# Windowed attention and a GELU network in one kernel: the division of the exponentials on GpSimd in all batches, their halves by one instruction over a range

## The chip, the core and the metric

The kernel runs on one core of a Trainium2 chip. The metric is the device time of one execution in microseconds. The kernel before was timed in three runs: 938.73, 940.12 and 943.64 us, median 940.12. One more execution was recorded by the hardware profiler.

## The reference, cut to what matters

Eight batches of eight heads attend over 576 tokens, each token to itself and the 127 before it, with a linear bias per head. The result goes through a network of two matrix products with a GELU between them.

```python
scores = scale * q @ k.T                         # B=8, H=8, S=576, D=64
scores = where((rel >= 0) & (rel < 128), scores - slope[h] * |rel|, -1e9)
attn = exp(scores - max(scores)); attn = attn / (sum(attn) + 1e-9)
x = (attn @ v).reshape(B * S, 512)
h = x @ w_in                                     # 512 x 2048
out = (0.5 * h * (1 + erf(h / sqrt(2)))) @ w_out # 2048 x 512
```

All of it is in float32. The kernel keeps that precision on 16-bit products: a number is split into a high half (its float16) and a low half (what is left, again float16), and a product takes three matrix products, high by high, high by low and low by high.

## The kernel before, in words

A batch has four units, one for each pair of heads. A unit's scores are nine groups of 128 rows by 192 keys, written s (two buffers). They fall into two ranges, EVEN with five groups and ODD with four; a range is the grain of the softmax.

**The softmax of batch 0** (`softmax_first`, L460 to L481). TensorE makes the scores in float32; VectorE takes the maxima (L469); ScalarE takes the exponentials with their sums z (L475); VectorE adds 1e-9 and inverts z (L478, L479) and multiplies each group by its 1/z (L481), into `e_main` for units 0 and 2 and into the space of `vbuf` for units 1 and 3. `turn` then transposes a unit's nine groups on TensorE (L496, with filler products of L490 ahead) and ScalarE evicts them to `et` (L498). `weigh` multiplies by v (`av`, L559), ScalarE writes the high half of `x` (L572) and VectorE the low half (`low_part`, recorded as L149).

**The softmax of the other batches** (`softmax`, L500 to L524). The exponentials go back into s in place (L510). In batches 1 and 2 ScalarE writes the high halves, one group at a time (L517); from batch 3 on GpSimd does (L519). VectorE computes the low halves, one group at a time, s * (1/z) - high (L149). Both halves go to `e_main`, of which there is one, and a DMA transposes each range to `et` (L522).

**Weights.** While batch 0's attention runs, the eight pieces of w_in come by DMA as 64-bit words. ScalarE and VectorE turn them into float32 (`zi`; ScalarE L190 and L192, VectorE L195, L196, L199) and split them into halves `wi` (ScalarE L207, VectorE L149). For the scale of two pieces their largest magnitudes are reduced over the partitions by GpSimd (`partition_all_reduce`, L114, in four steps called stw, one for each two pieces; in the listings they are stw_659, stw_686, stw_715 and stw_744). The same reduction serves v of batch 0 (stv) ahead of them, and q, k, v of batch 1 and w_out (stq, stv, stwo) after them. VectorE takes each result up in L115.

**The network.** Tile t is 512 tokens. `mlp_in` (L600) makes 16 blocks h of features from x; ScalarE applies GELU (L626 from tile 1 on), GpSimd and VectorE make the halves (L627, L149); `mlp_out` (L661) makes the output. In tile 0 the halves are made without GpSimd. The attention of batch b is laid between the steps of tile b - 1. The last two tiles use a form with seven products in place of eight.

**What sets the order.** The program is written in the order of the source with priorities, and a scheduler lays out each engine's queue before the run. Each engine then works through its queue strictly in that order. GpSimd has its routines in two libraries: `partition_all_reduce` is in library 1, `tensor_scalar` in library 0, and memset needs neither. Where the queue goes from a routine of one library to one of the other, the builder puts in an instruction that exchanges the library. In the listings it is a row `ISA` without a tile; the profile has it as MODIFY_POOL_CONFIG, in two parts. Before, the queue exchanges twice: to library 1 ahead of stv, and back to library 0 ahead of the first L627 in tile 1.

Of the kernel before, what the change touches and what calls it, by code (L numbers as in the profile page):

```python
# [14 lines left out]
AF = mybir.ActivationFunctionType  # L15
ALU = mybir.AluOpType
# [42 lines left out]
def attention_gelu_mlp(  # L59
# [10 lines left out]
    nc = tc.nc  # L70
# [389 lines left out]
    def softmax_first(st):  # L460

        u, s = st.u, st.s
        st.nmax = nmax = small([P, NG], f"nmax{u}", 2, tag="nmax")
        st.z = z = small([P, NG], f"z{u}", 2, tag="z")
        e = e_first[st.hp % 2]
        st.et = et = pool.tile([P, NG * 2, P], F32, tag=f"et{st.hp % 2}", name=f"et{u}", bufs=1)
        for r, c, banks in ((EVEN, slice(0, W), BANKS[0:3]), (ODD, slice(QB, 256), BANKS[3:5])):
            for bank in banks:
                nc.vector.tensor_reduce(  # L469
                    out=nmax[:, bank[0] : bank[-1] + 1], in_=st.ps[bank][:, 0 : len(bank), 0:W], axis=AX.X,  # L470
                    op=ALU.max, negate=True,
                )
            for bank in banks:
                for n, i in enumerate(bank):
                    nc.scalar.activation(  # L475
                        s[:, i, :], st.ps[bank][:, n, 0:W], AF.Exp, bias=nmax[:, i : i + 1], accum_out=z[:, i : i + 1]
                    )
            nc.vector.tensor_scalar_add(z[:, r], z[:, r], 1e-9)  # L478
            nc.vector.reciprocal(z[:, r], z[:, r])  # L479
            for i in range(r.start, r.stop):  # L480
                nc.vector.tensor_scalar_mul(e[:, i, c], s[:, i], z[:, i : i + 1])  # L481

    def turn(st):

# [15 lines left out]
    def softmax(st):  # L500
        u, s = st.u, st.s
        st.nmax = nmax = small([P, NG], f"nmax{u}", 2, tag="nmax")
        st.z = z = small([P, NG], f"z{u}", 2, tag="z")
        e = e_main
        st.et = et = pool.tile([P, NG * 4, P], F16, tag=f"et{st.hp % 2}", name=f"et{u}", bufs=1)
        for r, c, banks in ((EVEN, slice(0, W), BANKS[0:3]), (ODD, slice(QB, 256), BANKS[3:5])):
            nc.vector.tensor_reduce(out=nmax[:, r], in_=s[:, r], axis=AX.X, op=ALU.max, negate=True)  # L507
            with tc.high_priority(EXP_AHEAD):
                for i in range(r.start, r.stop):
                    nc.scalar.activation(  # L510
                        s[:, i, :], s[:, i, :], AF.Exp, bias=nmax[:, i : i + 1], accum_out=z[:, i : i + 1]
                    )
            nc.vector.tensor_scalar(z[:, r], z[:, r], 1e-9, 2.0 ** -E_SHIFT, op0=ALU.add, op1=ALU.mult)
            nc.vector.reciprocal(z[:, r], z[:, r])
            for i in range(r.start, r.stop):
                if st.b < 3:
                    nc.scalar.activation(e[:, i, 0, c], s[:, i], AF.Copy, scale=z[:, i : i + 1])  # L517
                    continue
                nc.gpsimd.tensor_scalar(e[:, i, 0, c], s[:, i], z[:, i : i + 1], 1.0, op0=ALU.mult, op1=ALU.mult)  # L519
            for i in range(r.start, r.stop):  # L520
                low_part(e[:, i, 1, c], s[:, i], z[:, i : i + 1], e[:, i, 0, c])
            nc.sync.dma_start_transpose(  # L522
                et[:, r.start * 4 : r.stop * 4, :], e[:, r].rearrange("p g h k -> p (g h k)")
            )  # L524
# [601 lines left out]
    for t in range(1, NTILE):  # L1126
# [26 lines left out]
        for step in range(2 * NFC):  # L1153
# [8 lines left out]
            if step in at:  # L1162
                hp, i = at[step]
# [63 lines left out]
```

## Time and profile before

| | us |
|---|---|
| median of three runs | 940.12 |
| lowest and highest run | 938.73, 943.64 |
| span of the profiled execution, first to last instruction | 936.4 |
| TensorE busy in it | 900.2 |
| VectorE busy | 737.2 |
| ScalarE busy | 555.9 |
| GpSimd busy | 199.0 |

The runs' times are whole executions, while the span goes from the first instruction to the last; the profiled execution's own whole time isn't listed apart. The median lies 3.7 us above the span, and that is taken as what lies around it. In rows of the profile, PE is TensorE, PEld its loading of weights, DVE VectorE, ACT ScalarE, POOL GpSimd and SP the engine that issues the DMAs; a q behind a name is the engine's queue. A row of the timeline has its start, its duration, engine, line, operation, written tile and read tiles, shapes and count, and in brackets the idle time before it with what ended it. A row of groups has count, busy time and the mean duration of one in ns. A row of windows has the stretch and its length, then the busy time of each engine with its instructions.

### The profile page before, as it was taken

What the parts mean: (1) busy time and instruction counts of PE and PEld (TensorE: products, weight loads), DVE (VectorE), ACT (ScalarE), POOL (GpSimd) and SP (SyncE); (2) the same over time, 40 slices, a digit from 0 to 9 for tenths busy, and PEclk for the clock granted to TensorE, in tenths of its full rate; (3) what the DMA queues carried; (4) which work ended last, traced back from release to release, by engine and by line L of the source; (5) the groups of instructions that cost most, each with busy time, mean ns of one, the idle gap of its engine ahead of it and who ended that gap; (6) DMA issues with size and microseconds to landing.
All of it is one profiled execution on the core that took longest, in us unless ns stands there. A gap on an engine that the chain in (4) does not pass through costs nothing.

```text
span 936.4 us, 18792 instructions
## 1 busy us (share of the span) xinstructions
PE 900.2 (96%) x7500; PEld 487.0 (52%) x7500; DVE 737.2 (79%) x1445; ACT 555.9 (59%) x1175; POOL 199.0 (21%) x412
## 2 busy tenths in 40 slices
PE   7969999779999899999999999999999999999998
PEld 3544444434454445444454445444444444488887
DVE  6898989779876877678767877687646898999771
ACT  5977958777673566256435643575465545744760
POOL 1010000013201443135303531164114540000000
PEclk9989999999999999999999999999999999999999
DMA  9518433872456133614562446224402351001001
GB/s 319 215 46 298 173 107 74 199 203 57 86 137 157 36 66 78 197 36 76 97 164 69 62 102 176 69 51 83 104 13 51 71 84 46 1 12 35 1 1 46
DMA packets 173512, 91.26 MB, mean 97 GB/s; under 512 B 132592, under 2 KB 155248, under 8 KB 173296
## 3 DMA queue, kind: packets, MB, share of 16 engines
q1 hardware_dynamic: 173424, 90.06, 38.6%
q8 instruction: 59, 0.97, 0.4%
q14 instruction: 29, 0.24, 0.1%
HBM read 46.53 MB, written 9.44 MB: 60 GB/s over the span
## 4 chain that ended last, share of the span: by engine, by line
PE 53%; DVE 19%; ACT 8%; DMA 4%; issue 3%; SPq 1%; POOL 0%; POOLq 0%; DVEq 0%; ACTq 0%
PE o L661 22%; PE h L600 17%; PE av L559 3%; PE sc L415 3%; DMA v<-vp 2%; ACT s L510 2%; PE u L860 2%; PE u_out L947 2%; DVE g L149 2%; DVE e_main L149 2%; DVE nmax L507 1%; PE v L860 1%; DMA et<-e_main 1%; DVE stv L217 1%; DVE s L437 1%
## 5 line engine op out<-in xcount | busy, mean ns | idle before, releaser
L600 PE MATMUL h<-x,wi 128*128 128x512 f16 x1536 | 341.1, 380 | 6.1 <-ACT g L626 3.1
L600 PEld LDWEIGHTS <-wi 128*128 128x128 f16 x1536 | 147.5, 98 | 184.7 <-issue 9.0
L661 PE MATMUL o<-wo,g 128*128 128x512 f16 x936 | 213.0, 380 | 1.1 <-DVE wo L149 1.1
L661 PEld LDWEIGHTS <-g 128*128 128x128 f16 x1248 | 117.2, 98 | 141.5 <-issue 2.3
L510 ACT ACTIVATE s<-s,nmax 128x192 f32<-128x192 f32 x252 | 111.2, 442 | 96.9 <-DVE nmax L507 93.3
L627 POOL TENSOR_SCALAR g<-g,sg 128x512 f16<-128x512 f32 x96 | 77.9, 817 | 192.0 <-ACT g L626 189.8
L149 DVE SCALAR_TENSOR_TENSOR e_main<-s,z,e_main 128x192 f16<-128x192 f32 x252 | 107.0, 468 | 13.1 <-POOL e_main L519 8.9
L519 POOL TENSOR_SCALAR e_main<-s,z 128x192 f16<-128x192 f32 x180 | 93.0, 534 | 86.9 <-issue 31.3
L626 ACT ACTIVATE g<-h,gs 128x512 f32<-128x512 f32 x96 | 63.9, 687 | 74.5 <-PE h L600 51.8
L149 DVE SCALAR_TENSOR_TENSOR g<-g,sg,g 128x512 f16<-128x512 f32 (+1 forms) x112 | 90.3, 824 | 21.0 <-POOL g L627 19.4
L415 PE MATMUL sc<-kbuf,qbuf 64*64 64x192 f16 (+1 forms) x1656 | 74.8, 263 | 9.2 <-DMA kbuf<-kp 4.5
L437 DVE SCALAR_TENSOR_TENSOR s<-sc,cs,bias_h 128x384 f32<-128x384 f32 x112 | 63.8, 608 | 12.2 <-PE sc L415 12.0
L661 PE MATMUL o<-wo_first,g 128*128 128x512 f16 x312 | 71.8, 379 | 0.1
L507 DVE TENSOR_REDUCE nmax<-s 128x5 f32<-128x960 f32 (+1 forms) x56 | 58.6, 1046 | 2.2 <-POOL s L442 0.2
L442 POOL MEMSET s<- 64x128 f32 (+1 forms) x112 | 19.1, 171 | 186.7 <-DVE s L437 186.1
L572 ACT ACTIVATE x<-av,cx 128x448 f16<-128x448 f32 (+6 forms) x52 | 23.5, 474 | 58.0 <-PE av L559 57.9
L415 PEld LDWEIGHTS <-qbuf 64*64 64x64 f16 x1512 | 36.0, 106 | 38.4 <-issue 36.9
L559 PE MATMUL av<-et,vbuf 128*64 128x128 f16 (+1 forms) x1680 | 44.1, 211 | 6.4 <-DMA et<-e_main 6.3
L559 PEld LDWEIGHTS <-vbuf 128*64 128x64 f16 x1680 | 41.0, 111 | 16.6 <-issue 11.3
L510 ACT ACTIVATION_READ_ACCUMULATOR s<-s,nmax 128x1 f32 x252 | 47.1, 187 | 0.0
L510 ACT ACT_TABLE_LOAD x29 | 37.2, 1283 | 7.9 <-DVE square L120 7.4
L947 PEld LDWEIGHTS <-g 128*128 128x128 f16 x384 | 37.6, 98 | 4.6
(268 smaller groups left out, 1159.7 us busy)
## 6 DMA issues: line engine op xcount, KB each, us to landing
v<-vp SPq DMA_DIRECT2D x32, 320.0 KB, 5.5
out<-ob SPq DMA_DIRECT2D x34, 256.0 KB, 2.3
raw<-w_in SPq DMA_DIRECT2D x8, 1024.0 KB, 13.7
raw<-w_out SPq DMA_DIRECT2D x8, 1024.0 KB, 5.1
q<-qp SPq DMA_DIRECT2D x7, 1152.0 KB, 6.2
k<-kp SPq DMA_DIRECT2D x7, 1152.0 KB, 6.3
qbuf<-qp SPq DMA_DIRECT2D x4, 288.0 KB, 4.9
kbuf<-kp SPq DMA_DIRECT2D x4, 288.0 KB, 5.2
```

Of the source, the lines that this page charges most:

```text
L149: nc.vector.scalar_tensor_tensor(out=dst, in0=src, scalar=scale, in1=high, op0=ALU.mult, op1=ALU.subtract)
L415: nc.tensor.matmul(ps[bank][o, n, 0:W], a, m, start=(i == 0), stop=(i == len(terms) - 1 and b > 0), skip_group_check=True,)
L437: nc.vector.scalar_tensor_tensor(out=s[:, bank[0] : bank[0] + k, :], in0=ps[bank][:, 0:k, 0:W], scalar=cs, in1=bias.broadcast_to([P, k, W] ...
L507: nc.vector.tensor_reduce(out=nmax[:, r], in_=s[:, r], axis=AX.X, op=ALU.max, negate=True)
L510: nc.scalar.activation(s[:, i, :], s[:, i, :], AF.Exp, bias=nmax[:, i : i + 1], accum_out=z[:, i : i + 1])
L519: nc.gpsimd.tensor_scalar(e[:, i, 0, c], s[:, i], z[:, i : i + 1], 1.0, op0=ALU.mult, op1=ALU.mult)
L559: nc.tensor.matmul(av[r, (j - blocks[0]) * QB : (j - blocks[0] + len(js)) * QB], v32s[b][:, hp, kb, r] if b < EXACT else vbuf[:, vi, hp, k ...
L600: nc.tensor.matmul(ph, wi[n][:, a, cc, k * P : (k + 1) * P], x[:, cc, b, :], start=(i == 0), stop=(i == 3 * NCC - 1),)
L626: nc.scalar.activation(g32, ph, AF.Gelu, scale=gsc[t, n])
L627: nc.gpsimd.tensor_scalar(g[:, r, 0], g32, gsg[t, n], 1.0, op0=ALU.mult, op1=ALU.mult)
L661: nc.tensor.matmul(o, both[:, a, c], wo[n][:, b, k, :], start=(fc == first and i == 0), stop=(fc == last and i == 2),)
L947: nc.tensor.matmul(ps[name][:, tb], f(d, a)[:, k, tb * P : (tb + 1) * P], w(d, b, k), start=first, stop=True, skip_group_check=True,)
```

## The change

In batch 0 GpSimd multiplies the groups by 1/z, in place of VectorE. In all other batches GpSimd multiplies s by 1/z in place, in float32; then one ScalarE instruction copies the range to the high halves, and one VectorE instruction subtracts it from s to the low halves. From batch 3 on GpSimd had done the multiplication already, with the high halves as its output.

```diff
@@ softmax_first
             for i in range(r.start, r.stop):
-                nc.vector.tensor_scalar_mul(e[:, i, c], s[:, i], z[:, i : i + 1])
+                nc.gpsimd.tensor_scalar(e[:, i, c], s[:, i], z[:, i : i + 1], 1.0, op0=ALU.mult, op1=ALU.mult)
@@ softmax
             for i in range(r.start, r.stop):
-                if st.b < 3:
-                    nc.scalar.activation(e[:, i, 0, c], s[:, i], AF.Copy, scale=z[:, i : i + 1])
-                    continue
-                nc.gpsimd.tensor_scalar(e[:, i, 0, c], s[:, i], z[:, i : i + 1], 1.0, op0=ALU.mult, op1=ALU.mult)
-            for i in range(r.start, r.stop):
-                low_part(e[:, i, 1, c], s[:, i], z[:, i : i + 1], e[:, i, 0, c])
+                nc.gpsimd.tensor_scalar(s[:, i], s[:, i], z[:, i : i + 1], 1.0, op0=ALU.mult, op1=ALU.mult)
+            nc.scalar.copy(e[:, r, 0, c], s[:, r])
+            nc.vector.tensor_tensor(out=e[:, r, 1, c], in0=s[:, r], in1=e[:, r, 0, c], op=ALU.subtract)
```

The lines after it move up by three: L597 is what was L600, L556 what was L559, L516 the new multiplication.

The queue of GpSimd in batch 0, before. It holds the reductions of v (stv) and of the weights (stw) and three memsets of pads:

```order
L114 ISA
L114 ISA stv_307<-stv_307 128x1
L114 ISA stw_659<-stw_659 128x2
L377 MEMSET kbuf 128x2x128
L114 ISA stw_686<-stw_686 128x2
L448 MEMSET e_main 128x10x64
L114 ISA stw_715<-stw_715 128x2
L449 MEMSET e_main 128x8x64
L114 ISA stw_744<-stw_744 128x2
L114 ISA stq_1141<-stq_1141 128x2
```

The same place after, up to the second weight reduction; `e_main` here is unit 0's output and `vbuf` unit 1's:

```order
L481 TENSOR_SCALAR e_main<-s_0_135,z_0_173 128x192 x5
L114 ISA
L114 ISA stv_307<-stv_307 128x1
L481 ISA
L481 TENSOR_SCALAR e_main<-s_0_135,z_0_173 128x192 x4
L114 ISA
L114 ISA stw_659<-stw_659 128x2
L481 ISA
L481 TENSOR_SCALAR vbuf<-s_1_202,z_1_278 128x192 x9
L377 MEMSET kbuf 128x2x128
L114 ISA
L114 ISA stw_686<-stw_686 128x2
```

The multiplications stand between the reductions, and with them the exchanges. The rest of batch 0 goes on in this way: exchange, nine groups of unit 2 and four of unit 3, the memset of L448, exchange, stw_715, exchange, the last five groups of unit 3, exchange, stw_744. From the first multiplication to stw_744 there are nine exchanges. One more stands ahead of the multiplications of batch 1, so that the whole program has eight more than before.

VectorE's queue before, around the last weight reduction's take-up (L115 of stw_744); x_367 is x of tile 0, and its rows here are the low halves of units 2 and 3:

```order
L149 SCALAR_TENSOR_TENSOR x_367<-av_2_0_572,scv_313,x_367 128x512
L196 SCALAR_TENSOR_TENSOR zi_745<-zi_745,raw_131 128x1024
L212 TENSOR_SCALAR pww<-stw_715 128x2
L195 TENSOR_SCALAR zo_818,stwo<-zo_818 128x1024
L196 SCALAR_TENSOR_TENSOR zi_745<-zi_745,raw_133 128x1024
L115 TENSOR_SCALAR stw_744<-stw_744 128x2
L149 SCALAR_TENSOR_TENSOR x_367<-av_3_0_633,scv_313,x_367 128x512
L199 SCALAR_TENSOR_TENSOR zi_745<-raw_131,zi_745 128x1024
```

The same place after:

```order
L196 SCALAR_TENSOR_TENSOR zi_745<-zi_745,raw_133 128x1024
L115 TENSOR_SCALAR stw_744<-stw_744 128x2
L199 SCALAR_TENSOR_TENSOR zi_745<-raw_131,zi_745 128x1024
L149 SCALAR_TENSOR_TENSOR x_367<-av_2_0_572,scv_313,x_367 128x512
L212 TENSOR_SCALAR pww<-stw_715 128x2
L199 SCALAR_TENSOR_TENSOR zi_745<-raw_133,zi_745 128x1024
```

The low half of unit 2 now stands behind the take-up of the last weight reduction; before it stood ahead of it. TensorE's first block h of tile 0 reads it.

## The prediction

> **What bounds the kernel now.** I read the page's busy shares first, then the windows by stage, then the timelines of TensorE and GpSimd up to 210 us, the groups, and the DMA issues.
>
> ```profile
> PE 900.2 (96%) x7500; PEld 487.0 (52%) x7500; DVE 737.2 (79%) x1445; ACT 555.9 (59%) x1175; POOL 199.0 (21%) x412
> core 0: us, PE busy (x) PEld busy (x) DVE busy (x) ACT busy (x) POOL busy (x), PEclk, DMA share, GB/s
> 20.00:80.00 60.00, 48.89 (x374) 30.40 (x373) 55.24 (x132) 48.86 (x108) 5.60 (x7) 0.89 0.50 174
> 80.00:140.00 60.00, 60.00 (x292) 27.62 (x291) 54.10 (x90) 49.54 (x84) 2.70 (x6) 1.00 0.50 175
> 140.00:220.00 80.00, 67.21 (x685) 34.55 (x678) 69.09 (x146) 59.75 (x142) 7.99 (x21) 1.00 0.62 147
> 220.00:860.00 640.00, 636.20 (x5397) 322.52 (x5396) 501.58 (x984) 349.08 (x757) 180.11 (x364) 1.00 0.36 80
> ```
>
> TensorE is the bound in all but two stretches. From 220 to 860 us it idles 3.8 us of 640, so an instruction more or less on another engine there is worth nothing until it uses up its slack. From 140 to 220 us it idles 12.8 us (batch 1's attention), and from 20 to 80 us 11.1 us (batch 0's). In the latter stretch VectorE is busy 55 of 60 us. Batch 0's attention ends thus:
>
> ```profile
> 70.03 3.00 PE L559 MATMUL av<-et,v 128*64 128x128 f32 x36 [3.49 <-ACT et L498]
> 72.97 17.21 PE L600 MATMUL h<-x,wi 128*128 128x512 f16 x75
> ```
>
> From 72.97 us on TensorE runs without a gap until past 140 us. So the time of the change is decided by when the first h can start, and then by what batch 1 gives back or takes. GpSimd's part in it:
>
> ```profile
> 14.34 1.24 DVE L481 TENSOR_SCALAR e_main<-s,z 128x192 f32<-128x192 f32 x5
> 1.59 0.29 POOL masks.py:199 TENSOR_SCALAR_AFFINE_SELECT adders<-adders 128x128 bf16<-128x128 bf16 x1 [0.29 <-POOL kbuf L301]
> 19.37 0.38 POOL L114 PARTITION_ALL_REDUCE stv<-stv  x1 [16.36 <-DVE z L478]
> 26.11 1.26 POOL L114 PARTITION_ALL_REDUCE stw<-stw  x1 [6.36 <-DMA raw<-w_in]
> 30.30 0.31 POOL L377 MEMSET kbuf<- 128x256 f16 x1 [2.92 <-PE sc L415]
> 49.38 1.26 POOL L114 PARTITION_ALL_REDUCE stw<-stw  x1 [18.77 <-DVE zi L195]
> 52.99 0.63 POOL L448 MEMSET e_main<- 128x640 f16 x1 [2.35 <-PE tp L496]
> 66.82 1.32 POOL L114 PARTITION_ALL_REDUCE stw<-stw  x1 [9.45 <-DVE zi L195]
> 204.85 3.16 POOL L627 TENSOR_SCALAR g<-g,sg 128x512 f16<-128x512 f32 x3 [27.42 <-ACT g L626]
> L627 POOLq MODIFY_POOL_CONFIG  x2: 4/4/4, 177.5 to 177.5; - x2
> ```
>
> GpSimd only reduces here, and every reduction waits for data. Its two exchanges of libraries (ahead of 19.37 and of 204.85) lie in idle stretches of 16.36 and 27.42 us. The exchange itself is recorded with 4 ns a part, which is its issue; whether the new routines are there by then, the trace can't say.
>
> **The change part by part.** First, the moved multiplications of batch 0, and the rows for the rest:
>
> ```profile
> L481 DVE TENSOR_SCALAR vbuf<-s,z 128x192 f32<-128x192 f32 x18 | 4.6, 326 | 0.0
> L481 DVE TENSOR_SCALAR e_main<-s,z 128x192 f32<-128x192 f32 x18 | 4.5, 316 | 0.0
> L519 POOL TENSOR_SCALAR e_main<-s,z 128x192 f16<-128x192 f32 x180 | 93.0, 534 | 86.9 <-issue 31.3 <-ACT s L510 27.6 <-ACT x L572 25.4
> L149 DVE SCALAR_TENSOR_TENSOR e_main<-s,z,e_main 128x192 f16<-128x192 f32 x252 | 107.0, 468 | 13.1 <-POOL e_main L519 8.9 <-ACT e_main L517 4.0
> L517 ACT ACTIVATE e_main<-s,z 128x192 f16<-128x192 f32 x72 | 26.5, 443 | 7.1 <-DMA et<-e_main 4.0 <-issue 1.6 <-ACT s L510 1.5
> L747 DVE TENSOR_TENSOR room<-wo 128x1024 f32<-128x1024 f16 x6 | 7.4, 1229 | 0.0
> L207 ACT ACTIVATE wi<-zi,sww 128x1024 f16<-128x1024 f32 x8 | 8.8, 1151 | 2.0 <-DVE sww L144 2.0
> ```
>
> VectorE loses 36 multiplications, 4.6 + 4.5 = 9.1 us of a stretch in which it is nearly full. GpSimd gains 36 at 0.534 us, 19.2 us, in a stretch in which it was busy for 5.6 of 60. By themselves these would let h start earlier: 9.1 us less on VectorE, against 9 x (0.534 - 0.25) = 2.5 us more for the last unit (0.25 us is VectorE's step, 1.24 us for five). Call that -6.6 us at best and 0 at worst.
>
> Second, the exchanges. The multiplications stand between the reductions, so the queue exchanges nine times up to the last weight reduction, and now not in idle time but one behind another. Let one cost c. It has no row, only bounds: from below the 0.29 us ahead of the affine_select, a gap that holds an exchange (it may have been one to a library already there); from above the 16.36 us that hid one completely. Between such ends I go by the nearest thing that the trace has, if an exchange has to fetch anything: a DMA of some hundred KB (the libraries' size isn't known):
>
> ```profile
> pair<-alibi SPq DMA_DIRECT2D x1, 288.0 KB, 5.6
> pair<-alibi SPq DMA_DIRECT2D x1, 96.0 KB, 3.0
> raw<-w_in SPq DMA_DIRECT2D x8, 1024.0 KB, 13.7
> ```
>
> A few hundred KB land in 3.0 to 5.6 us, 1 MB under load in 13.7 us. I take c = 5.5 us, with 4 to 8 as its likely ends and 0.3 and 16 as its bounds.
>
> The Trainium skill, "GPSIMD Engine Reference", section 2.1 (Instruction dispatch), says that the first call into a freshly loaded library pays a code load of about 6 us (5.95 measured) that no instruction of the profile shows; the sum below with 5.95 would be 3.6 us higher, and no run so far shows the load.
>
> The chain on GpSimd, counted from 14.34 us, where the first multiplication can start: five multiplications, exchange, stv 0.38, exchange, four, exchange, stw 1.26, exchange, nine, memset 0.31, exchange, stw 1.26. That is 18 x 0.534 + 0.38 + 1.26 + 0.31 + 1.26 = 12.8 us and five exchanges, so the second weight reduction ends at 27.2 + 5c. Then the memset of `e_main`'s pads (L448) waits for unit 2's transposes. These wait for VectorE and ScalarE work that follows the reduction in their queues:
>
> ```profile
> L199 DVE SCALAR_TENSOR_TENSOR zi<-raw,zi 128x1024 int32<-128x1024 int32 x8 | 9.8, 1223 | 0.0
> L190 ACT ACTIVATE zi<-raw 128x1024 f32<-128x1024 f32 x8 | 9.3, 1186 | 2.4 <-DVE zi L235 1.3 <-DMA raw<-w_in 1.1
> L498 ACT COPY et<-tp 128x512 f32<-128x512 f32 x16 | 9.0, 618 | 1.6 <-PE tp L496 1.6
> L149 DVE SCALAR_TENSOR_TENSOR x<-av,scv,x 128x512 f16<-128x512 f32 x4 | 3.0, 752 | 0.5 <-ACT x L572 0.5
> ```
>
> On VectorE two L199 (2.4), one low half of x (0.75) and a dozen small ones (about 3); on ScalarE two L207 (2.3), four L190 (4.7), and about 4 for exponentials, half an x and evictions: an estimate of 17 us. One exchange and 13 multiplications of GpSimd run beside that (c + 6.9), so this wait hides them. The rest: memset 0.63, exchange, stw 1.3, exchange, five multiplications 2.7, exchange, stw 1.32. The last weight reduction ends at 27.2 + 17 + 6 + 8c = 50.2 + 8c, counting three exchanges behind the wait and five ahead of it. At c = 5.5 that is 94.2 us, against 68.1 before.
>
> Who waits for it: the exchange to library 1 and stw_744 have no reader that needs them at once, but VectorE's queue holds the take-up L115 of stw_744 ahead of the low half of unit 2, which every h reads. Behind L115 come one L199 (1.2) and that low half (0.75); TensorE then has nine products and the rest of the last av (3.0 us row, about 2.5 of it) ahead. So h starts, in terms of before, at 50.2 + 4.8 + 8c = 55 + 8c, against 72.97. The shift is 8c - 18: +26 us at 5.5, +14 at 4, +46 at 8, and zero at c = 2.2, below which VectorE is the bound as before.
>
> Third, the other batches. For each range of five, five low halves at 0.468 become one subtraction of 960 elements, 1.15 us by L747's 1.229 for 1024; ScalarE gains one copy of 1.08 us by L207's rate (56 copies, about 55 us) and loses the 26.5 us of L517. GpSimd gains 72 multiplications. The way from 1/z to the transposing DMA becomes serial: 2.7 + 1.1 + 1.15 = 4.9 us against about 2.6 before, 2.3 us longer in each range. From batch 2 on that is covered by TensorE's work and costs nothing; if the cover were too short, it would cost up to 2.3 us a range. In batch 1 the DMA sets the pace, since `e_main` is free for the next range only when its transposition is done:
>
> ```profile
> 166.68 6.02 DMA et<-e_main
> 176.96 6.65 DMA et<-e_main
> ```
>
> GpSimd no longer waits for that, as it writes s, and what stays between two DMAs is copy and subtraction, 2.2 us, as much as before. VectorE has about 36 x 0.468 - 8 x 1.04 = 8.5 us less there and has done some of its w_out work while it waited in batch 0. I take -5 us, between 0 and -9 of the 12.8 us of idle time. The exchange ahead of batch 1's multiplications lies behind a memset and may show once; its c is inside that range.
>
> Sum: 26 - 5 = +21 us on a span of 936.4, so 957.4. The median of the runs lies 3.7 us above the span, which gives 961 us.
>
> **The rivals.** One more row, the spread (fastest, median, slowest) of the multiplication that follows the second exchange:
>
> ```profile
> L627 POOL TENSOR_SCALAR g<-g,sg x96: 684/772/1819, 204.8 to 735.1; 128x512 f16<-128x512 f32 x96
> ```
>
> The first rival ends on the other side: an exchange is nearly free. For it speaks the 0.29 us gap and that the row shows 4 ns; against it, that the one at 177.5 us is followed by three L627 in 3.16 us, 1.05 each, where the fastest takes 0.684, so that something was late even after 27 us of idle time.
>
> Then VectorE's 9.1 us decide: -5 us at the start of h and -4 in batch 1, 931 us. The turn is at c = 2.2, or 2.8 with batch 1's gain counted.
>
> The second: c is about 3, by the 96 KB row. The shift is +6, batch 1 gives it back, and the time is 941 us, no change.
>
> The third: the exchanges are cheap, but the longer way in batch 1 is exposed in each of its eight ranges, 8 x 2.3 = +18, less the 5 us at the start of h: 953 us. Against it speaks that the DMA sets the pace there.
>
> **How the numbers follow.** I give the costly exchange (c over 4) 0.74, the free one 0.16, the middle one 0.07, the exposed batch 1 0.03. The forecast is the first's, 961 us; its own range goes from c = 4 with the full gain in batch 1 (949) to c = 8 with none (986). The range over all cases reaches down to 932, half of the free case, and up to 986, past which dearer exchanges under the weights' DMA traffic lie with 0.1. A change under 0.5%, 4.7 us, can't be told from none here. The free case is faster by more in nearly all its parts: 0.14. Same: 0.09. Slower: 0.77.
>
> **What would show it right or wrong.** Right: gaps on GpSimd behind each exchange in batch 0, of 4 us or more, with the data long there; the last weight reduction near 94 us; the first h near 99 us; TensorE's idle time in 220 to 860 us, shifted, still about 4 us; a window of batch 1 with less idle time than 12.8. Wrong: reductions that start as soon as their data are there, the first h before 73 us, or idle time of TensorE before av in batches 2 to 7.

## The result and the profile after

The changed kernel takes 988.8 us (median of four runs, 985.8 to 989.5) against 939.5 us before (938.7 to 943.6): 1.051 times as long, 95% interval 1.049 to 1.053. The forecast was 961 us, with 932 to 986 as its range: slower, as forecast, but by 49 us in place of 21. The profiled execution has a span of 986.6 us against 936.4.

The busy shares of the page, and the windows of the three stages (up to the first h, batch 1, the rest), first of the changed kernel, then of the kernel before. The columns are the window and its length, busy time and instructions of TensorE, its weight loads, VectorE, ScalarE and GpSimd, then TensorE's granted clock, the DMA share and GB/s.

```profile
PE 916.5 (93%) x7500; PEld 494.6 (50%) x7500; DVE 692.5 (70%) x1213; ACT 579.4 (59%) x1159; POOL 252.9 (26%) x520
20.00:98.00 78.00, 49.20 (x335) 31.32 (x328) 42.28 (x86) 44.32 (x102) 21.60 (x39) 0.73 0.31 110
98.00:329.00 231.00, 209.65 (x1619) 101.74 (x1619) 182.31 (x326) 147.99 (x293) 60.04 (x123) 0.95 0.51 136
329.00:975.00 646.00, 634.16 (x5386) 347.96 (x5385) 455.66 (x776) 375.57 (x736) 166.99 (x340) 1.00 0.31 69
```

```profile
20.00:73.00 53.00, 41.89 (x346) 27.37 (x345) 48.70 (x121) 44.56 (x103) 5.60 (x7) 0.89 0.43 155
73.00:289.00 216.00, 203.21 (x1596) 98.66 (x1596) 187.84 (x381) 158.20 (x349) 21.02 (x51) 1.00 0.57 149
289.00:925.00 636.00, 631.85 (x5385) 346.83 (x5384) 487.25 (x915) 342.11 (x696) 169.78 (x340) 1.00 0.31 69
```

The first stage is 25 us longer, the second 15, the third 10. VectorE, the engine that the change relieves, was busy for 48.7 of 53 us in the first stage and is now for 42.3 of 78: it waits. Of the 50.2 us that the span grew, 33.9 are idle time of TensorE and 16.3 are its *busy* time (916.5 against 900.2, for the same 7500 matmuls). Some 14 of these 16.3 lie in the first two stages (7.3 and 6.4), where TensorE was given a lower clock, 0.73 and 0.95 in place of 0.89 and 1.00. GpSimd up to batch 1 (start, duration, instruction, and in brackets its idle time and what ended it):

```profile
22.43 0.38 POOL L114 PARTITION_ALL_REDUCE stv<-stv  x1 [6.41 <-issue]
30.86 1.62 POOL L481 TENSOR_SCALAR e_main<-s,z 128x192 f32<-128x192 f32 x4 [8.05 <-ACT et L498]
38.35 0.37 POOL L114 PARTITION_ALL_REDUCE stw<-stw  x1 [5.87 <-issue]
45.83 6.65 POOL L481 TENSOR_SCALAR vbuf<-s,z 128x192 f32<-128x192 f32 x9 [7.10 <-DVE zi L196]
58.79 0.37 POOL L114 PARTITION_ALL_REDUCE stw<-stw  x1 [6.06 <-issue]
66.19 5.59 POOL L481 TENSOR_SCALAR e_main<-s,z 128x192 f32<-128x192 f32 x9 [7.02 <-DVE z L479]
...
74.28 0.63 POOL L448 MEMSET e_main<- 128x640 f16 x1
80.80 0.37 POOL L114 PARTITION_ALL_REDUCE stw<-stw  x1 [5.89 <-issue]
88.08 2.02 POOL L481 TENSOR_SCALAR vbuf<-s,z 128x192 f32<-128x192 f32 x5 [6.91 <-DVE zi L196]
96.03 0.37 POOL L114 PARTITION_ALL_REDUCE stw<-stw  x1 [5.92 <-issue]
...
176.48 8.64 POOL L516 TENSOR_SCALAR s<-s,z 128x192 f32<-128x192 f32 x13 [7.17 <-ACT wo L207]
```

Here the exchange of libraries has become visible. GpSimd stands still for 5.9 to 6.4 us ahead of each of batch 0's reductions, and for about 7 us (once 8.05) ahead of every group of multiplications. The instructions named as releasers are not the reason: the last of the z that the groups at 45.83 and 66.19 read were there at 40.3 and 64.4. TensorE around the first h and in batch 1, with the kernel before's one row for the same 192 h and the products behind them below it:

```profile
98.44 4.00 PE L597 MATMUL h<-x,wi 128*128 128x512 f16 x9 [4.06 <-DVE x L149]
102.37 2.09 PE L556 MATMUL av<-et,v 128*64 128x128 f32 x26
104.39 8.59 PE L597 MATMUL h<-x,wi 128*128 128x512 f16 x39
...
143.66 0.41 PE L415 MATMUL sc<-kbuf,qbuf 64*64 64x192 f16 x8 [1.46 <-ACT kbuf L372]
145.67 0.43 PE L415 MATMUL sc<-kbuf,qbuf 64*64 64x192 f16 x8 [1.60 <-DVE qbuf L149]
149.47 1.59 PE L415 MATMUL sc<-kbuf,qbuf 64*64 64x192 f16 x26 [3.36 <-DVE kbuf L149]
151.51 6.71 PE L597 MATMUL h<-x,wi 128*128 128x512 f16 x24 [0.45 <-ACT g L614]
...
189.42 1.69 PE L415 MATMUL sc<-kbuf,qbuf 64*64 64x192 f16 x28 [7.05 <-DVE s L437]
```

```profile
72.97 42.47 PE L600 MATMUL h<-x,wi 128*128 128x512 f16 x192
115.27 13.04 PE L654 MATMUL o<-zo,g 128*128 128x512 f32 x30
```

Two things are new beside the late start. Batch 1's first scores (`sc`) now stand *ahead* of the last 24 h and wait 6.4 us for the split of q and k, where the kernel before had all 192 h and 15 products first (30 rows of `o`, since a product in float32 has two). And later TensorE waits 7.05 us for VectorE. Last, TensorE's waits from 330 us on (total, times, longest), and the new softmax's groups:

```profile
PE av L556 <- DMA et<-e_main: 6.5, 5, 2.2
PE sc L415 <- DVE s L437: 2.1, 1, 2.1
PE h L597 <- ACT g L623: 1.8, 1, 1.8
```

```profile
L516 POOL TENSOR_SCALAR s<-s,z 128x192 f32<-128x192 f32 x252 | 130.1, 535 | 109.7 <-DVE z L514 85.7 <-ACT x L569 8.9 <-ACT wo L207 7.2
L518 DVE TENSOR_TENSOR e_main<-s,e_main 128x960 f16<-128x960 f32 (+1 forms) x56 | 59.7, 1065 | 24.5 <-ACT e_main L517 24.4
L517 ACT CAST e_main<-s 128x960 f16<-128x960 f32 (+1 forms) x56 | 50.3, 906 | 49.7 <-POOL s L516 49.7
```

The prices of the new instructions were well estimated (0.535, 1.07 and 0.91 us, each copy and subtraction a mean over ranges of five and of four). Their place was not: TensorE waits in front of `av` for the transposing DMA. In the same stage of the kernel before, from 289 us on, no such wait is listed; the largest totals there are:

```profile
PE h L600 <- ACT g L626: 3.1, 2, 2.4
PE sc L415 <- DVE s L437: 0.6, 1, 0.6
```

In all TensorE idles 11.8 us in this stage (646.00 - 634.16), where it idled 4.2 before; the prediction had expected about 4 again, and had named idle time before `av` as a sign of being wrong.

The experiments are compared by three lengths, read off the starts of h on TensorE's timeline: the start of the first h, the time from there to the first h of tile 2 (which holds all of batch 1's attention), and from there to the end of the last matmul. A gate in the table is the h of tile 0 behind whose result batch 1's split of q and k may start; it is h 5 unless a row says otherwise, and its runs are explained below.

| kernel | median, us | first h | batch 1's stages | the rest |
|---|---|---|---|---|
| before | 939.5 | 73.0 | 215.9 | 643.9 |
| changed | 988.8 | 98.4 | 230.9 | 653.6 |
| batch 0 back on VectorE | 947.0 | 73.3 | 218.8 | 650.1 |
| batch 0 alone | 977.4 | 99.3 | 227.4 | 644.5 |
| batches 1 and 2 alone | 939.0 | 69.8 | 218.7 | 642.2 |
| batches 3 to 7 alone | 943.8 | 71.3 | 216.3 | 650.6 |
| exchanges alone | 962.7 | 87.0 | 223.1 | 645.9 |
| batch 0 on GpSimd, no exchange | 945.1 | 70.1 | 224.1 | 644.5 |
| the same, VectorE multiplies | 959.0 | 68.4 | 238.6 | 646.7 |
| batch 0 alone, scores held | 985.4 | 98.7 | 233.2 | 644.6 |
| batch 0 alone, gate 7 | 970.0 | 101.7 | 219.5 | 643.8 |
| before, gate 7 | 942.4 | 73.1 | 218.9 | 644.8 |
| batches 3 to 7, halves by group | 942.2 | 72.0 | 216.1 | 648.7 |
| no exchange, gate 9 | 938.8 | 69.6 | 219.8 | 644.5 |
| multiplied twice | 976.5 | 71.4 | 215.9 | 680.5 |
| copies aside | 939.9 | 72.1 | 218.7 | 646.5 |
| whole change, gate 7 | 980.9 | 102.0 | 224.1 | 648.8 |

The first h of kernels with the same batch 0 comes between 69.8 and 73.3 us, so a difference of 3 us in one such column is not to be read; the medians and their intervals carry the verdicts.

### The profile page after: what moved, and what is told of

Read it like the earlier page. It is cut to its first block, busy times and chain, and to the rows that moved or that the text cites. A ratio compares the mean times of both kernels' runs of the same rounds, so it can differ in the third digit from the quotient of the medians.

```text
span 986.6 us, 18726 instructions
## 1 busy us (share of the span) xinstructions
PE 916.5 (93%) x7500; PEld 494.6 (50%) x7500; DVE 692.5 (70%) x1213; ACT 579.4 (59%) x1159; POOL 252.9 (26%) x520
## 4 chain that ended last, share of the span: by engine, by line
PE 44%; DVE 15%; ACT 9%; DMA 7%; POOL 6%; issue 4%; SPq 1%; POOLq 0%; DVEq 0%; ACTq 0%
PE o L658 17%; PE h L597 11%; POOL s L516 4%; DMA v<-vp 4%; ACT s L510 4%; PE u_out L944 3%; PE av L556 3%; DMA et<-e_main 2%; PE u L857 2%; DVE g L149 2%; DVE s L437 2%; DVE nmax L507 2%; PE sc L415 2%; DVE stv L217 2%; PE v L857 2%
## 5 line engine op out<-in xcount | busy, mean ns | idle before, releaser
L597 PE MATMUL h<-x,wi 128*128 128x512 f16 x1536 | 343.8, 382 | 9.3 <-DVE x L149 4.1
L597 PEld LDWEIGHTS <-wi 128*128 128x128 f16 x1536 | 147.8, 98 | 189.4 <-issue 15.4
L658 PEld LDWEIGHTS <-g 128*128 128x128 f16 x1248 | 117.8, 98 | 141.3 <-issue 2.4
L516 POOL TENSOR_SCALAR s<-s,z 128x192 f32<-128x192 f32 x252 | 130.1, 535 | 109.7 <-DVE z L514 85.7
L415 PE MATMUL sc<-kbuf,qbuf 64*64 64x192 f16 (+1 forms) x1656 | 79.3, 274 | 24.9 <-DVE s L437 12.2
L517 ACT CAST e_main<-s 128x960 f16<-128x960 f32 (+1 forms) x56 | 50.3, 906 | 49.7 <-POOL s L516 49.7
L518 DVE TENSOR_TENSOR e_main<-s,e_main 128x960 f16<-128x960 f32 (+1 forms) x56 | 59.7, 1065 | 24.5 <-ACT e_main L517 24.4
L556 PE MATMUL av<-et,vbuf 128*64 128x128 f16 (+1 forms) x1680 | 44.3, 211 | 8.9 <-DMA et<-e_main 6.5
L556 PEld LDWEIGHTS <-vbuf 128*64 128x64 f16 x1680 | 41.4, 111 | 18.9 <-issue 12.6
L149 DVE SCALAR_TENSOR_TENSOR x<-av,cx,x 128x448 f16<-128x448 f32 (+6 forms) x52 | 25.2, 489 | 22.4 <-ACT x L569 22.1
```

The lines of the kernel that those rows point to most:

```text
L149: nc.vector.scalar_tensor_tensor(out=dst, in0=src, scalar=scale, in1=high, op0=ALU.mult, op1=ALU.subtract)
L415: nc.tensor.matmul(ps[bank][o, n, 0:W], a, m, start=(i == 0), stop=(i == len(terms) - 1 and b > 0), skip_group_check=True,)
L516: nc.gpsimd.tensor_scalar(s[:, i], s[:, i], z[:, i : i + 1], 1.0, op0=ALU.mult, op1=ALU.mult)
L518: nc.vector.tensor_tensor(out=e[:, r, 1, c], in0=s[:, r], in1=e[:, r, 0, c], op=ALU.subtract)
L556: nc.tensor.matmul(av[r, (j - blocks[0]) * QB : (j - blocks[0] + len(js)) * QB], v32s[b][:, hp, kb, r] if b < EXACT else vbuf[:, vi, hp, k ...
L597: nc.tensor.matmul(ph, wi[n][:, a, cc, k * P : (k + 1) * P], x[:, cc, b, :], start=(i == 0), stop=(i == 3 * NCC - 1),)
```

## The experiments

**The parts of the change.** Four kernels, each with a part of the change. The first is the changed kernel with the line of batch 0 taken back:

```diff
-                nc.gpsimd.tensor_scalar(e[:, i, c], s[:, i], z[:, i : i + 1], 1.0, op0=ALU.mult, op1=ALU.mult)
+                nc.vector.tensor_scalar_mul(e[:, i, c], s[:, i], z[:, i : i + 1])
```

> The changed kernel with batch 0's multiplications back on VectorE, so that GpSimd only reduces up to the first h. Theory A (three separate costs: batch 0's exchanges +25.5, batch 1's own new way +15, batches 2 to 7's longer way +10): first h at 73 us again and about 964 us. Rival B (one delay that is passed on: batch 1 is late only because batch 0 pushed VectorE's and ScalarE's weight work back into it): first h at 73 us, batch 1 as before or better, about 949 us or less.

Measured: 947.0 us, 1.008 (1.006 to 1.010) of before. The lateness up to the first h is gone, and with it 12 of batch 1's 15 us, though batch 1 still had all of its new softmax. The second is the kernel before with only that line changed the other way:

> The kernel before with only batch 0's multiplications on GpSimd. Theory A: first h near 98 us and the rest as before, about 965 us. Rival B: the lateness comes back as a loss in batch 1 as well, about 980 us. A later first h with batch 1's work done in the wait would show a gain in batch 1 and 955 us.

Measured: 977.4 us, 1.041 (1.038 to 1.044). Batch 0 alone costs 38 us: 26 up to the first h and 11.5 more in batch 1, whose own code is that of before. Rival B holds in this point: batch 1's loss comes from batch 0.

The third and the fourth are the kernel before with the new softmax only where the condition holds, `st.b < 3` in the third, `st.b >= 3` in the fourth:

```diff
+            if st.b < 3:
+                for i in range(r.start, r.stop):
+                    nc.gpsimd.tensor_scalar(s[:, i], s[:, i], z[:, i : i + 1], 1.0, op0=ALU.mult, op1=ALU.mult)
+                nc.scalar.copy(e[:, r, 0, c], s[:, r])
+                nc.vector.tensor_tensor(out=e[:, r, 1, c], in0=s[:, r], in1=e[:, r, 0, c], op=ALU.subtract)
+            else:
...
```

> The kernel before with the new softmax (multiplication on GpSimd in place, one copy, one subtraction) in batches 1 and 2 alone. Theory A: batch 1 loses about 15 us by its exchange and its serial way, about 955 us. Rival B: batch 1 by itself loses nothing and gains up to 9 us, 930 to 940 us.

> The kernel before with the new softmax in batches 3 to 7 alone; there GpSimd multiplied already, so only the in-place target and the single copy and subtraction are new. Theory A: the longer way outlasts TensorE's cover in some ranges, about 946 to 949 us, with idle time of TensorE ahead of av. Rival B (those gaps come from batch 0's lateness or its buffers): 939 us.

Measured: 939.0 us for batches 1 and 2, 1.001 (0.999 to 1.003): no change, and neither the loss of theory A nor the gain that the prediction and rival B hoped for. For batches 3 to 7, 943.8 us, 1.0057 (1.0039 to 1.0074): a loss of half of one per cent, with the idle time ahead of `av` that theory A named. TensorE's waits from 390 to 900 us in this kernel:

```profile
PE av L565 <- DMA et<-e_main: 3.8, 4, 2.2
PE av L565 <- DVE s L437: 1.5, 1, 1.5
PE av L565 <- DVE room L753: 0.5, 1, 0.5
```

So theory A is right for batches 3 to 7 and rival B for batch 1. The changed kernel's 49 us are batch 0's 38, batches 3 to 7's 5 and some 6 that appear only together.

**What makes batch 0 late.** The kernel before, its multiplications on VectorE, with one GpSimd instruction of a single column ahead of each of the five reductions:

```diff
+            if ticks:
+                nc.gpsimd.tensor_scalar(ticks.pop(), stat[:, 0:1], 1.0, 1.0, op0=ALU.mult, op1=ALU.mult)
             nc.gpsimd.partition_all_reduce(stat, stat, P, bass_isa.ReduceOp.max)
```

> The kernel before, multiplications on VectorE, with one GpSimd instruction of a single column (its result is read by nobody) ahead of each of batch 0's five reductions over partitions, so that each reduction has an exchange of libraries right before it, with its data already there. The order of TensorE's work is that of before, word for word. If an exchange costs 5.9 us as the changed kernel's rows say, four weight reductions each end about 6 us later, the first h comes 10 to 24 us later, and the total is 949 to 975 us; if the lateness there was GpSimd's multiplications and not exchanges, 940 us. On batch 1: if the loss after a late start is handed on by the lateness itself, h to h of batch 1's two stages grows by a third to a half of the shift again; if it comes from the other order of TensorE's work (scores of batch 1 ahead of the last 24 h), these two stages stay at 216 us within 3.

Measured: 962.7 us, 1.025 (1.023 to 1.027), with the first h at 87.0. GpSimd's timeline in it (`tick` is the single column; it is ready for the reduction when it ends):

```profile
37.02 0.19 POOL L118 TENSOR_SCALAR tick<-stw 128x1 f32<-128x1 f32 x1 [8.23 <-DVE zi L201]
43.12 0.37 POOL L119 PARTITION_ALL_REDUCE stw<-stw  x1 [5.91 <-issue]
...
57.41 0.20 POOL L118 TENSOR_SCALAR tick<-stw 128x1 f32<-128x1 f32 x1 [13.67 <-DVE zi L200]
63.84 0.37 POOL L119 PARTITION_ALL_REDUCE stw<-stw  x1 [6.22 <-issue]
...
71.51 0.19 POOL L118 TENSOR_SCALAR tick<-stw 128x1 f32<-128x1 f32 x1 [6.72 <-DVE z L484]
77.41 0.37 POOL L119 PARTITION_ALL_REDUCE stw<-stw  x1 [5.71 <-issue]
```

An instruction of 0.19 us on one column costs GpSimd 5.7 to 6.2 us behind it, with the reduction's data already there (these are three of the five; the first and the last took 8.6 and 9.8 us). This is the exchange by itself. Batch 1's stages take 223.1 us, which is outside the 216 within 3 that the theory of the order asked for, and by its size fits the rival. Where those 7.2 us lie speaks against the rival, though. TensorE's next rows in this kernel:

```profile
97.35 5.08 PE L605 MATMUL h<-x,wi 128*128 128x512 f16 x15 [3.04 <-DVE x L154]
105.02 28.65 PE L605 MATMUL h<-x,wi 128*128 128x512 f16 x132 [2.58 <-ACT g L622]
...
136.61 13.04 PE L659 MATMUL o<-zo,g 128*128 128x512 f32 x30
```

From the first h to the first `o` it takes 49.6 us, against 115.27 - 72.97 = 42.3 before: the last reduction ends at 96.5, so the later weights and x are not there when h asks for them. From that `o` to the first h of tile 2 it is 173.5 us in both kernels (136.6 to 310.1; 115.3 to 288.8). The lateness is not handed on, once TensorE has its order of before.

The reverse: batch 0's multiplications on GpSimd, and the five reductions by small VectorE instructions (`over_partitions` without `early`), so that nothing is exchanged; and a control with the same reductions and VectorE's multiplications.

> Batch 0's multiplications on GpSimd as in the changed kernel (the softmax of the other batches as before), and batch 0's five reductions over partitions by small VectorE instructions in their place, so that GpSimd has no exchange up to batch 1. If the exchanges made the first h late, it comes between 66 and 80 us (VectorE loses 9.1 us and gains five reductions of about ten small instructions each), and the total is 930 to 950 us; if the 36 multiplications at 0.534 us did, it stays near 90 us and the total near 965 us.

> The kernel before with batch 0's five reductions by small VectorE instructions, multiplications on VectorE: the control of the run with GpSimd's multiplications and the same reductions. By the prediction's working the multiplications by themselves are worth 0 to 6.6 us, so this one should be 0 to 7 us slower than that run; if GpSimd's slower multiplications cost time without any exchange, it is faster.

Measured: 945.1 us, 1.007 (1.005 to 1.009), and 959.0 us, 1.022 (1.020 to 1.024). With the same 36 multiplications on GpSimd and no exchange the first h comes at 70.1 us. The multiplications are not what is late. Beside the control they are even worth 14 us, twice what was expected, but not at the first h (68.4 there): VectorE has the reductions on top in these two kernels, and in the control the weights of later h come late (TensorE waits once for 12.4 us on L207). The control also has batch 1's first scores ahead of the last 24 h, as the changed kernel has, so the 14 us are not the price of the multiplications alone.

**What batch 1 loses.** The order in which a scheduler laid out the queues differs between the two kernels around batch 1. On ScalarE the split of q and k (L372) stands thus before, with the eviction of h 14 (`h_14`) behind it:

```
L372 ACTIVATE qbuf<-q_1_868,scq_1149 128x2304
L372 ACTIVATE kbuf<-k_1_869,scq_1149 128x2304
L619 ACTIVATE g_3_1057<-g_0_6_1059,sg_6_765 128x256
L613 ACTIVATE g_3_1057<-h_14_1086,gs_6_763 128x256
```

and thus in the changed kernel, ahead of the evictions of h 11, 12 and 13, and with weight work between:

```
L372 ACTIVATE qbuf<-q_1_868,scq_1149 128x2304
L372 ACTIVATE kbuf<-k_1_869,scq_1149 128x2304
L190 ACTIVATE zo_1080<-raw_1042 128x1024
L192 ACTIVATE raw_1042<-raw_1042 128x1024
L610 ACTIVATE g_2_971<-h_11_1020,gs_4_734 128x256
```

The first attempt to undo this held only TensorE's part: a copy of one column that lets batch 1's first scores start when the last h is out.

```diff
             ps[bank] = psum.tile([P, 2, 256], F32, tag=tag, name=f"sc{u}_{bank[0]}", bufs=4)
+            if b == 1 and hp == 0:
+                nc.scalar.copy(ps[bank][:, 0, 0:1], hold)
...
+    hold = low_of_first(15)
     pwm, s2 = weights_out_scale()
```

> Only batch 0's multiplications on GpSimd (the run at 977 us), with a one-column copy on ScalarE that lets batch 1's first scores start only when the last h of tile 0 is out, so that TensorE has all 192 h first, as before the change. If the order made batch 1 lose its 11.5 us, 966 to 970 us; if VectorE's and ScalarE's lateness did, whatever the order, 975 to 979 us.

Measured: 985.4 us, 1.050 (1.048 to 1.052), slower than either theory allowed and than the kernel it is built on (977.4). TensorE had all 192 h first, but now the h waited:

```profile
PE h L602 <- ACT g L619: 11.6, 3, 9.3
PE av L561 <- DMA et<-e_main: 6.9, 1, 6.9
```

The split still stood ahead of the evictions on ScalarE, whose results free the buffers for the next h. Holding TensorE to its order is therefore not enough; what this run left as it was is the place of the split in ScalarE's and VectorE's queues. The second attempt moved that, by the column that gates it:

```diff
-            split_qk(1, low_of_first(5))
+            split_qk(1, low_of_first(7))
```

> Only batch 0's multiplications on GpSimd (the run at 977 us), with the column that holds back the q and k split of batch 1 taken from h 7 in place of h 5. The split then stands behind most of tile 0's evictions in ScalarE's and VectorE's queues, as it does in the kernel before, and all 192 h stand ahead of batch 1's scores. If the place of the split in the queues costs batch 1 its 11.5 us, the two stages of batch 1 come back to 216 to 221 us and the total to 966 to 970 us; if the late start costs it in any order, 975 us or more.

> The kernel before with the same changed gate alone (h 7 in place of h 5), nothing on GpSimd: the control. If the gate only corrects an order that the change spoiled, it gives nothing here: 936 to 945 us. If it is a gain of its own, it is 930 us, and its effect beside GpSimd's multiplications proves nothing about the order.

Measured: 970.0 us with batch 0 alone, 7.3 us less than with gate 5, and 942.4 us for the control, 1.0039 (1.0026 to 1.0052) of before, so a small loss there. TensorE's row in the former shows the h running through after the first few:

```profile
117.22 31.24 PE L600 MATMUL h<-x,wi 128*128 128x512 f16 x144 [0.92 <-ACT g L617]
```

Batch 1's stages take 219.5 us against 218.9 in the control, where they took 227.4 with gate 5. The two kernels differ by 28 us now, which is their first h (101.7 against 73.1). With the gate at h 7 a late start costs batch 1 next to nothing (0.6 us); the other order costs it 8 us. The gate has a price of its own, 3 us where nothing is late (218.9 against 215.9), so that 3.6 of the 11.5 us are not undone. Applied to the whole change:

> The whole change with the gate of batch 1's q and k split at h 7 in place of h 5. If the place of the split costs the whole change what it costs with batch 0's part alone, 7 to 11 us come back: 977 to 982 us, with the two stages of batch 1 near 220 us in place of 231. If batch 1's loss there is its own new softmax behind a late start, 986 to 990 us.

Measured: 980.9 us, 1.046 (1.044 to 1.049), 8 us less, with 224.1 us in batch 1's stages. Against the 219.5 of batch 0's part with the same gate 4.6 us remain. Both kernels start late, so these belong to the new softmax behind the late start. Two rows go with them, GpSimd's first multiplications of batch 1, and TensorE's wait for the freeing of the scores' banks between 150 and 327 us, which with batch 0's part alone is 3.3 us:

```profile
185.65 2.02 POOL L516 TENSOR_SCALAR s<-s,z 128x192 f32<-128x192 f32 x5 [7.42 <-DVE z L513]
PE sc L415 <- DVE s L437: 8.5, 4, 3.3
```

The z of these multiplications was there at 179.7, so that 6 us of the exchange are not covered by the wait for z. In the changed kernel it is 4.3 us (172.2 to 176.48), with the new softmax in batches 1 and 2 alone 1.8 (138.8 to 140.57). That this exchange causes the waits of the scores was read from the queues; no run takes it out by itself. And the kernel without exchanges, with the gate at h 9:

> Batch 0's multiplications on GpSimd, its reductions by VectorE, so no exchange (the run at 945 us), and the gate of the q and k split at h 9, which puts all 192 h and 22 of the products behind them ahead of batch 1's scores. If the order of the split and not the start of h cost that run its 10 to 14 us in the stage of tile 0, it comes to 931 to 938 us, at or below the kernel before; if VectorE's work does, 943 to 948 us.

Measured: 938.8 us, 1.000 (0.9985 to 1.0011). Six of the 945.1 come back, not all that was hoped for; no kernel tried here beats the one before.

**What batches 3 to 7 lose.** Three kernels, in which TensorE's order is that of before but for the place of some `av`: in the first it stands one product earlier in three places, in the second 4 to 13 products later in five; in the third it is where it was. The new softmax there with copy and subtraction group by group, each right behind its multiplication:

```diff
                 nc.gpsimd.tensor_scalar(s[:, i], s[:, i], z[:, i : i + 1], 1.0, op0=ALU.mult, op1=ALU.mult)
-            nc.scalar.copy(e[:, r, 0, c], s[:, r])
-            nc.vector.tensor_tensor(out=e[:, r, 1, c], in0=s[:, r], in1=e[:, r, 0, c], op=ALU.subtract)
+                nc.scalar.copy(e[:, i, 0, c], s[:, i])
+                nc.vector.tensor_tensor(out=e[:, i, 1, c], in0=s[:, i], in1=e[:, i, 0, c], op=ALU.subtract)
```

> The new softmax in batches 3 to 7 (GpSimd multiplies in place), but copy and subtraction group by group in place of one instruction each over the range, so that they follow each multiplication; TensorE's order is that of the run with batches 3 to 7 alone (943.8 us). If the longer serial way from 1/z to the transposing DMA costs those batches their 5 us, it comes back: 938 to 940 us. If the load on ScalarE and VectorE does, it stays or grows, since both now have more instructions: 944 to 950 us.

Measured: 942.2 us, 1.0045 (1.0027 to 1.0062), between the two theories and not to be told from 943.8 with certainty. TensorE's waits from 390 to 900 us are of another kind:

```profile
PE h L606 <- ACT g L632: 1.6, 4, 0.6
PE av L565 <- DMA et<-e_main: 1.4, 2, 1.0
```

The wait for the DMA fell from 3.8 to 1.4 us, and h waits for ScalarE in its place. So two kernels that load one side alone: the kernel before with every multiplication of batches 3 to 7 done twice, and the kernel before with a copy to a place aside for every group.

```diff
-                nc.gpsimd.tensor_scalar(e[:, i, 0, c], s[:, i], z[:, i : i + 1], 1.0, op0=ALU.mult, op1=ALU.mult)
+                for _ in range(2):
+                    nc.gpsimd.tensor_scalar(e[:, i, 0, c], s[:, i], z[:, i : i + 1], 1.0, op0=ALU.mult, op1=ALU.mult)
```

> The kernel before with every group's multiplication on GpSimd in batches 3 to 7 done twice, to the same place: the way from 1/z to the transposing DMA gets up to 5 x 0.53 = 2.7 us longer in each range, about what the new softmax makes it longer, and ScalarE and VectorE have nothing more to do. If the way costs batches 3 to 7 their 5 us, 942 to 946 us with TensorE waiting for the DMA ahead of av; if the load on ScalarE and VectorE does, 938 to 940 us.

```diff
+            if st.b >= 3:
+                for i in range(r.start, r.stop):
+                    nc.scalar.copy(aside, s[:, i, 0:96])
             nc.sync.dma_start_transpose(
```

> The kernel before with nine more ScalarE copies (128x96, to a place that nobody reads) in each unit of batches 3 to 7: ScalarE has some 3 us more to do per unit, more than the two copies of the new softmax add, and the way to the DMA keeps its length. If load on ScalarE costs the 5 us, 942 to 946 us with TensorE's h waiting for the evictions of h; if the way does, 938 to 940 us.

Measured: 976.5 us, 1.040 (1.037 to 1.042), for the doubled multiplications, and 939.9 us, 1.0015 (1.0000 to 1.0029), for the copies. The rows of the first: its waits of TensorE, and its multiplications; and the copies of the second, 48 us more for ScalarE, above the new softmax's 40 copies at 0.91 us:

```profile
PE av L560 <- DMA et<-e_main: 19.1, 8, 3.8
PE h L601 <- ACT g L627: 6.8, 4, 2.4
...
L520 POOL TENSOR_SCALAR e_main<-s,z 128x192 f16<-128x192 f32 x360 | 181.2, 523 | 78.2 <-ACT s L510 34.1 <-ACT x L573 21.5 <-issue 16.9
```

```profile
L526 ACT CAST aside<-s 128x96 f16<-128x96 f32 x180 | 48.1, 267 | 3.4
```

The load on ScalarE is free, the way is not: with up to 2.6 us more in it (5 x 0.523 more multiplications, by the row) the kernel loses 37 us from tile 2 on (680.5 against 643.9), many times what was expected. GpSimd's queue also carries L628, and VectorE's low halves took 0.527 us each in place of 0.468 (121.8 us in place of 107.0 for all), so how much of the 37 us is the way alone was not separated. What is shown is that more work of GpSimd on the way costs time, with TensorE waiting for the DMA, though ScalarE and VectorE have no instruction more.

## Why the prediction went wrong in its size

Measured are 49 us where 21 were forecast. By the profiled execution, which grew by 50.2, the late first h came out as forecast, batch 1 is 20 us beyond its term of the sum, and batches 2 to 7 are 10 us beyond theirs.

**The late first h: right in its mechanism, with errors in the terms that nearly cancel.** Forecast was a shift of +26 us from eight exchanges at 5.5 us; measured are +25.5, with the last weight reduction ending at 96.4 (forecast 94.2). The exchange costs 5.9 to 6.4 us towards the reductions and 6.9 to 8.1 towards the multiplications, a mean of 6.5 for the eight that the sum counts, which alone would have made the last reduction 8 us later. The working had 17 us for a wait of GpSimd for unit 2's transposes, which was to hide the ninth exchange. No such wait is there (L448 starts at 74.28 right behind the multiplications): from the end of the second weight reduction to there GpSimd does that exchange and 13 multiplications itself, 15.1 us, 2 less than the wait. The other 4 us lie mostly in the reductions, which took 0.37 us where the sum had 1.26 to 1.32. From the last reduction to the first h it is 2.0 us (take-up, L199, low half) in place of 4.8, since the rest of the last `av` stands behind the first nine h and not ahead of them. That this part fits to 1 us is luck; that the first h has to wait for the exchanges one behind another is not. The price taken from a transfer of some hundred KB was of the right size, though no run shows that the exchange is such a transfer. The Trainium skill, "GPSIMD Engine Reference", section 2.1, gives about 6 us (5.95 measured) for the first call into a freshly loaded kernel; the reductions here agree with it (5.7 to 6.4 us, but for two at 8.6 and 9.8), and the multiplications lie a microsecond or two above it. It was the better estimate.

The rival of the free exchange is refuted by the one-column instruction, and the one of c near 3 by the same rows. The third, a longer way exposed in batch 1 by itself, is refuted by the kernel with the new softmax in batches 1 and 2 alone, which takes the time of before. The 4 ns of the exchange's own row say nothing of its price. One sum of the prediction is wrong: c = 4 with the full gain of 9 us in batch 1 gives 945 us; its 949 is the sum with a gain of 5. The range over all cases doesn't rest on it.

**Batch 1: wrong, -5 us forecast, +15.1 measured.** The step that failed is "In batch 1 the DMA sets the pace", with the gain from VectorE's 8.5 us less behind it. It took the order of the queues as given. What TensorE waited for in batch 1 was the split of q and k (6.4 us) and VectorE (10.1 us in three waits, the longest 7.05); no wait of `av` for that DMA is listed there. The change gave the scheduler a slower engine for batch 0's multiplications, and it laid the split of batch 1's q and k ahead of tile 0's evictions; TensorE then waited 6.4 us for that split, and ran at a lower clock behind it (the last 24 h in 6.71 us, 0.28 each). Gate 7 takes 6.8 us of the 15.1 back in the whole change and 7.9 in batch 0's part. Of the 8.3 that stay, 3 are what gate 7 costs by itself. Nearly all of the other 5 is the new softmax behind a late start (4.6). What fits it is the exchange ahead of batch 1's multiplications, which the prediction saw and put inside its range, and VectorE's queue: the subtraction of a range waits for ScalarE's copy, this for the range's five or four multiplications, and behind the subtraction on VectorE stand the instructions that free the scores' banks (the 7.05 us at 189.42); this was read from the queues and the waits, and no run has it by itself. The gain itself did not show: with the new softmax in batches 1 and 2 alone the time is that of before.

**Batches 2 to 7: wrong, 0 forecast, +9.7 measured.** The step that failed is "From batch 2 on that is covered by TensorE's work and costs nothing". The price that the prediction named for a broken cover, up to 2.3 us a range, would be 110 us over 48 ranges; the cover breaks at five places only, each up to 2.2 us, 6.5 us in all. Batches 3 to 7 alone account for 5 us. That the longer way can cost time is shown by the doubled multiplications, which also hold up GpSimd's other work; that it is *all* of those 5 us is argued, since shortening it group by group gave back the DMA's waits but not surely the time.

**A term was missing.** The windows showed TensorE's clock at 0.89 in the stretch with 11.1 us of idle time (and at 1.00 in the one with 12.8), and the prediction didn't ask what more idle time in batch 0 would do to it. Nine h after a wait of 4.06 us took 4.00 us, 0.44 each; 39 of them a little later took 8.59, 0.22 each. The granted clock was 0.50 from 98.4 to 102.4 us and 1.00 from 104.4 to 113. In the sum the lower clock is some 14 of the 16.3 us of TensorE's busy time, those of the first two stages; the forecast had nothing for them. The Trainium skill, "TensorE: Matmul & The Clock Gate", Why this matters for your kernels, warns of idle gaps over about 3 us between bursts of matmuls, since the clock falls back behind them; the trace agrees (4.06 us of idle, half speed).

## What to carry to other kernels

Between GpSimd's own elementwise instructions and its reductions over partitions lies an exchange of 6 to 7 us each way (here up to 9.8) whose time no row shows; keep them in separate stretches of its queue, or hide each exchange in time in which that engine waits anyway. Where a scheduler lays out the queues, read the new order one stage further than the edit, on the engines that the change doesn't touch: here a seventh of the loss lay in a split that moved ahead of other evictions on ScalarE. And before a step on the way to a transfer is made serial, look at how much slack TensorE's cover has at its tightest place, not at its mean idle time: 4 us of idle time in 640 still left places with less slack than the 2.3 us that the way was estimated to grow by.

## What the runs showed of the hardware

The exchange starts with the queue, not with the data: the `tick` at 57.41 had waited 13.7 us for its data and ran 0.1 us after they were there (57.3), so the exchange ahead of it had been done in the wait. In the kernel before both exchanges of the prediction's listing lie in such waits, of 16.4 and 27.4 us, which is why its trace hid their price. In the changed kernel it is paid at every change of direction, nine times up to 96 us, also towards routines that had run 14 us earlier (52.5 to 66.2). Towards elementwise instructions it is longer, 6.9 to 7.2 us and once 8.05, against 5.9 to 6.4 towards reductions. Of the five towards reductions in the run with exchanges alone three took 5.7 to 6.2 us and two 8.6 and 9.8, for a reason that was not found. Memory fills (L448 behind multiplications) run without one.
